# Infini-attention block with adaLN on one core: the value read-outs of a pair put in one group, the tile of row maxima padded to 128 columns

## The chip, the cores and the metric

The kernel runs on one core of a Trainium2 chip. The metric is the device time of one launch in microseconds (us). Three runs of the kernel before gave 856.10, 855.74 and 852.11 us, so the median is 855.74 us.

## The reference, cut to what matters

A transformer block over 2048 rows of width 512: layer norm with a shift and scale from a conditioning vector, an attention with 32 heads of width 16, a projection `wo`, a second layer norm, and a feed-forward part of width 1792 with a gelu. The attention works on four segments of 512 rows. Inside a segment it is a softmax over a masked score matrix; beside it a memory from the earlier segments is read out.

```python
mask = (ar[:, None] < ar[None, :]) * (-1e9)
for s in range(4):                                   # segments of 512 rows
    logits = einsum("bhqd,bhkd->bhqk", qs, ks) * scale + mask
    p = softmax(logits)
    a_dot = einsum("bhqk,bhkd->bhqd", p, vs)
    a_mem = (phi(qs) @ M) / (phi(qs) @ z + 1e-6)
    outs.append(g * a_mem + (1 - g) * a_dot)
    M, z = M + phi(ks)^T vs, z + sum(phi(ks))
```

## The kernel before, in words

The program has three stages. Stage A (about 0 to 195 us of the profile) makes q, k, v and the memory read-outs. The attention stage (about 195 to 512 us) works through the 4 x 32 = 128 matrices of scores, 512 x 512 each. The feed-forward stage takes the rest. The change touches the attention stage alone.

The attention stage runs over steps `P` = -4 to 65. A step stands for two heads (`NP` = 64 of them), and an even and the following odd step make a *pair* `Q` of four heads. For each head the scores are computed twice, on TensorE both times:

- the S parts (`s_part`, L615) give scores with rows on the partitions, only to find each row's maximum. S0 is two tiles of width 512, S1 two of 384; S2 holds two of 256 in one PSUM bank, S3 two of 128 in one bank. VectorE takes the maxima: `masked_max` (L608) for S0 to S2, an instruction that is followed by a read of the accumulator, and a plain reduction (`s_max`, L612) for S3 after the mask has been added by a matmul (`s_mask`, L645; M3 in the order). The S parts run four steps ahead of the rest.
- the T parts (`st_part`, L697) give the scores transposed, with the maximum already subtracted through three extra rows of the operand. T0 and T1 are 512 wide (one for each head), T2 and T3 384, T4 holds two of 256, T5 two of 128. ScalarE takes the exponential (L706, L717) and GpSimd zeroes the triangle (`causal`, L693). The results are the tiles `pt0` to `pt3`.

All S and T parts of a step take turns at six PSUM banks, `att0` to `att5` (`bank`, L601). A step uses twelve, so the banks come round twice in each step, and which part stands in which bank follows from the order of the tokens. A part can start only when the engine that read its bank last is done: VectorE for S, ScalarE for T.

The value read-out (`pv_part`, L722) multiplies `pt0` to `pt3` of a pair by V. Each of its four parts `j` is four matmuls onto 32 columns of the array each, side by side, and the profile shows each of these as two instructions (eight a part). They accumulate in the one bank `pv`, which ScalarE copies out (`pv_out`, L736).

Between the maxima and the T parts stand `m_rows` (L662), two small subtractions on VectorE that split the maxima in three bf16 terms in the tile `nm`; `m_put` (L668), a matmul that turns them into rows (48 columns wide); a copy to `ms` on ScalarE and a DMA of `ms` into the three extra rows of `qst`.

The projection after the attention (`wo_part`, L798) has 12 matmuls for each block of 128 rows; before the feed-forward stage they run in three runs of four pairs, one block in each pair. I call these pairs *projection pairs* and the others *plain pairs*.

The order of the work is written by hand, and every engine keeps to it. `PRM['order']` holds a string for the even and one for the odd step of each segment; `S`, `T` and `M` are parts, `c0` to `c9` are places where other work is hung in. `ap(pos, ...)` (L861) hangs work at step `pos // 10`, place `c(pos % 10)`. So `'pv'` with `[25, 0, 0, 512]` puts part 0 of pair `Q` at `20 Q + 25`, the place c5 of step `2Q + 2`. `wo`, `mput`, `pvout`, `den` and `mrows` work likewise. An L number is a line of the kernel before, as in its profile; in the changed kernel lines 40 to 592 stand three lines higher and the rest where it was.

Of the kernel before, what the change touches and what calls it, by code (L numbers as in the profile page):

```python
# [8 lines left out]
F32 = mybir.dt.float32  # L9
# [13 lines left out]
VROW = 560  # L23
EPS = 1e-5
PRM = {'order': ['S0 c0 c1 T0 T1 S1 c2 T2 c3 c4 c5 T3 S3 c6 M3 S2 c7 c8 c9 T4 T5',
# [9 lines left out]
 'turn': 2,  # L35
# [4 lines left out]
 'pvout': [35, 35, 35, 35],  # L40
 'mrows': [-19, -20, -20, -20],
 'mput': [-9, -14, -14, -14],
 'stacks': -64,
 'den': [84, 84, 84, 84],
 'dnl': 11,
# [1 line left out]
 'mix': [105, 105, 100, 103],  # L47
 'ohi': [110, 110, 110, 111],
 'olo': [110, 110, 110, 116],
 'wo': [[2, 10, 10, 10], [6, 10, 11, 11], [2, 10, 10, 11]],  # L50
 'woout': [10, 11, 11],
 'wox': [-23, -23, -23, -13],
 'mixu': 14,
# [50 lines left out]
def block_kernel(ctx: ExitStack, tc: tile.TileContext, x, wq, wk, wv, wo, betaq, betam,  # L104
                 w1, b1c, w2, b2, ccol, wmod, maskbd, mask8, out):
    nc = tc.nc
    v, act, pool, pe, sp = nc.vector, nc.scalar, nc.gpsimd, nc.tensor, nc.sync
# [6 lines left out]
    identb = per.tile([128, 128], BF16, name="identb")  # L114
# [12 lines left out]
    def copy(e, dst, src):  # L127
        if e == "a":
            act.activation(dst, src, AF.Copy)
        else:  # L130
            (v if e == "v" else pool).tensor_copy(dst, src)
# [94 lines left out]
    with ExitStack() as pa:  # L226
# [102 lines left out]
        for k in range(KB):  # L329
            for c in range(2):  # L330
                pe.matmul(ps[32 * c:32 * c + 32, :], sc[:, k:k + 1].to_broadcast([128, 32]), wms[c, k],
                          start=(k == 0), stop=(k == KB - 1))
# [6 lines left out]
        for ds in ((0,), (1, 2, 3)):  # L339
            cps = pst(f"cps{ds[0]}")  # L340
            for d in ds:
                pe.matmul(cps[:, 2 * d:2 * d + 2], row[:64, 128 * d:128 * d + 128] if d else row0, sel,
                          start=True, stop=True)
            n = slice(ds[0], ds[-1] + 1)
# [181 lines left out]
        for s in range(NSEG):  # L526
            for tok in PRM["A"][s].split():
                n = int(tok[1]) if len(tok) > 1 and tok[1].isdigit() else 0
# [53 lines left out]
    mm = psw.tile([128, 512], F32, name="mm")  # L582
# [3 lines left out]
    with ExitStack() as pb:  # L586
        sb = pb.enter_context(tc.tile_pool(name="sb", bufs=2, reuse_waits="tile"))
# [5 lines left out]
        wol = so.tile([128, KB, D], F32R, name="wol", bufs=1)  # L593

        nms, nss = {}, {}

        banks = {n: [pb_.tile([128, 512], F32, name=f"{n}{i}") for i in range(c)]
                 for n, c in (("att", 6), ("pv", 1))}
# [2 lines left out]
        def bank(n):  # L601
            turn[n] = turn.get(n, -1) + 1
            return banks[n][turn[n] % len(banks[n])]

        def s_mm(ps, P, h, i):
            pe.matmul(ps, q_of(P, h, i), k_of(P, h, 128 * (i + 1)), start=True, stop=True)  # L606

        def masked_max(dst, src, n):  # L608
            v.tensor_tensor_reduce(out=src, in0=src, in1=maskb[:, 512 - n:], scale=-1.0, scalar=-4 * NEG,  # L609
                                   op0=ALU.add, op1=ALU.min, accum_out=dst)  # L610
# [4 lines left out]
        def s_part(P, part):  # L615
            Q, p = P // 2, P % 2
            if p == 0 and part == 0:
                nms[Q] = sb.tile([128, 3, 16], F32, tag="nm", bufs=4, name=f"nm{Q}")
            nm = nms[Q][:, 0].rearrange("q (p h i) -> q p h i", p=2, h=2)
            if part < 2:  # L620
                i = 3 - part
                n = 128 * (i + 1)
                ps = [bank("att"), bank("att")]
                for h in range(2):
                    s_mm(ps[h][:, :n], P, h, i)
                for h in range(2):
                    masked_max(nm[:, p, h, i:i + 1], ps[h][:, :n], n)
            else:
                i = 3 - part
                n = 128 * (i + 1)  # L630
                ps = bank("att")
                pair = ps[:, :2 * n].rearrange("q (h n) -> q h n", h=2)
                if PRM["m"][2 * p + i]:
                    for h in range(2):
                        s_mm(pair[:, h, :], P, h, i)
                    for h in range(2):
                        masked_max(nm[:, p, h, i:i + 1], pair[:, h, :], n)
                    return
                pe.matmul(pair[:, 0, :], q_of(P, 0, i), k_of(P, 0, n), start=True, stop=False)
                pe.matmul(pair[:, 1, :], q_of(P, 1, i), k_of(P, 1, n), start=False, stop=False)  # L640
                pend.append((pair, nm[:, p, :, i:i + 1]))
# [11 lines left out]
        def q_of(P, h, i):  # L653
            return qst[P // 2 % NK][:96, 2 * (P % 2) + h, 128 * i:128 * i + 128]

        def k_of(P, h, n):
            return kst[P // 2 % NK][:96, 2 * (P % 2) + h, 0:n]

        def top(t):
            return t.bitcast(BF16).rearrange("q (n two) -> q n two", two=2)[:, :, 1]  # L660
# [6 lines left out]

        def m_put(Q):  # L668
            ns = nss.pop(Q)
            pe.matmul(mm[:48, :128], top(ns.rearrange("q c n -> q (c n)")), identb, start=True, stop=True)  # L670
            ms = sb.tile([48, 128], BF16, tag="ms", bufs=2, name=f"ms{Q}")
            copy(PRM["mse"], ms, mm[:48, :128])
            act.dma_start(qst[Q % NK][96:99], ms)
# [197 lines left out]
        for Q in range(32):  # L871
            z = Q // 8
            pv = PRM["pv"][z]
# [54 lines left out]
        for P in range(-LEAD, NP + 2):  # L928
            if P in PRM["w1at"]:
                stage_w1(2 * PRM["w1at"].index(P))  # L930
            for tok in PRM["order"][2 * min(P // 16, 3) + P % 2 if P >= 0 else 8 + P % 2].split():
                n = int(tok[1])
                if tok[0] == "S":
                    if P + LEAD < NP:
                        s_part(P + LEAD, n)
                elif tok[0] == "M":
                    s_mask()
                elif tok[0] == "T":
                    if 0 <= P < NP:
                        st_part(P, n)  # L940
                else:
                    for f, a in todo.pop((P, n), ()):
                        f(*a)
# [5 lines left out]
    with ExitStack() as pc:  # L949
        c1 = pc.enter_context(tc.tile_pool(name="c1", bufs=1, side="right", reuse_waits="tile"))  # L950
# [86 lines left out]
        c2 = pc.enter_context(tc.tile_pool(name="c2", bufs=1, reuse_waits="tile"))  # L1037
# [46 lines left out]
        for n in range(AHEAD, NSEG * FB + AHEAD):  # L1084
            s, f = divmod(n, FB)
# [77 lines left out]
```

## Time and profile before

| | us |
|---|---|
| median of the three runs | 855.74 |
| the profiled execution's own time | 852.17 |
| its span, first to last instruction | 850.4 |
| TensorE busy in the span | 811.8 (95%) |
| VectorE busy | 525.5 (62%) |
| ScalarE busy | 361.2 (42%) |
| GpSimd busy | 288.9 (34%) |

A row of a timeline gives the start, the length, the engine, the line, the operation, its tiles and shapes, and how often it was merged (x2). Matmuls overlap in the records: a matmul of width 512 lasts 0.38 us from start to end, but the next one starts 0.22 us after it. What a matmul costs TensorE is therefore read from start to start. The same holds for VectorE and ScalarE, where a read-out of the accumulator runs beside the next instruction. A row of the windows view gives a stretch of the span, and of each engine the busy time in it and the number of instructions, then the clock granted to TensorE.

### The profile page before, as it was taken

The numbers are of one execution on the slowest core, as the hardware profiler recorded it, in microseconds if no ns is written. First come the engines' busy times: TensorE is split into PE (matmuls) and PEld (weight loads), VectorE is DVE, ScalarE is ACT, GpSimd is POOL, SyncE is SP. The second block draws the span as 40 slices with busy tenths as digits, with TensorE's granted clock in tenths as the row PEclk, the third lists the DMA queues.
The fourth block names the chain that finished last, engine by engine and source line by source line (L and its number), as shares of the span: only waits on it lengthen the run. The fifth ranks groups of instructions, "written<-read, shape, count | busy, mean of one in ns | idle before, by whom it ended". The sixth has DMA issues, their size and how long they took to land.

```text
span 850.4 us, 13376 instructions
## 1 busy us (share of the span) xinstructions
PE 811.8 (95%) x4650; PEld 549.8 (65%) x4650; DVE 525.5 (62%) x1427; ACT 361.2 (42%) x730; POOL 288.9 (34%) x454
## 2 busy tenths in 40 slices
PE   6999999979999999999999899799999999999998
PEld 2777767836443455435544447688888888888887
DVE  5684676447999987897799727685442434233312
ACT  3554644522787865676687572142111211111110
POOL 1346367362367544567866561000000000000000
PEclk9999999989999999999999999899999999999999
DMA  9936747396465576666567466460030103002001
GB/s 338 325 133 228 255 166 235 108 296 199 113 176 167 150 218 189 202 191 200 174 176 217 133 182 205 155 203 30 21 99 1 49 2 99 1 0 75 26 1 49
DMA packets 83564, 123.01 MB, mean 145 GB/s; under 512 B 14116, under 2 KB 46244, under 8 KB 82984
## 3 DMA queue, kind: packets, MB, share of 16 engines
q1 hardware_dynamic: 81000, 120.19, 44.9%
q10 hardware_dynamic: 2496, 1.97, 0.7%
q8 instruction: 36, 0.59, 0.3%
q14 instruction: 32, 0.26, 0.1%
HBM read 75.60 MB, written 46.15 MB: 143 GB/s over the span
## 4 chain that ended last, share of the span: by engine, by line
PE 69%; DVE 13%; DMA 8%; issue 5%; ACT 3%; POOL 2%; SPq 0%; ACTq 0%; DVEq 0%; POOLq 0%
PE acc L1065 18%; PE f1b L984 16%; PE pv L731 6%; DVE att L609 6%; PE att L691 6%; PE att L606 4%; PE mm L804 4%; PE k L503 3%; PE q L503 2%; PE v L475 2%; PE nu L445 1%; DMA QD<-q 1%; DMA xt<-X2D 1%; DMA qst<-ms 1%; DVE nm L609 1%
## 5 line engine op out<-in xcount | busy, mean ns | idle before, releaser
L609 DVE CUSTOM_DVE_ANT_0 att<-att,maskb 128x512 f32<-128x512 f32 (+2 forms) x384 | 206.4, 580 | 13.8 <-PE att L606 11.6
L706 ACT ACTIVATE pt<-att 128x512 f32<-128x512 f32 (+1 forms) x256 | 126.0, 553 | 57.2 <-PE att L691 56.5
L987 ACT ACTIVATE gt<-f1b,b1t 128x512 f32<-128x512 f32 x56 | 38.4, 688 | 243.6 <-PE f1b L984 221.4
L694 POOL TENSOR_SCALAR_AFFINE_SELECT pt<-pt 128x256 f32<-128x256 f32 x256 | 100.2, 407 | 108.1 <-ACT pt L706 78.6
L137 DVE CAST gh<-gt 128x512 fp32r<-128x512 f32 x56 | 23.8, 426 | 156.7 <-ACT gt L987 153.8
L691 PE MATMUL att<-qst,kst 99*128 99x512 bf16 (+3 forms) x512 | 107.5, 300 | 9.1 <-DVE nm L609 3.3
L606 PE MATMUL att<-kst,qst 96*128 96x512 bf16 (+2 forms) x384 | 94.6, 327 | 1.6 <-DVE nm L613 1.2
L731 PE MATMUL pv<-pt,V 128*32 128x512 f32 (+2 forms) x992 | 88.2, 446 | 0.0
L1065 PE MATMUL acc<-w2h,gh 128*128 128x512 f32 (+1 forms) x224 | 87.2, 389 | 0.0
L1065 PE MATMUL acc<-w2l,gh 128*128 128x512 f32 (+1 forms) x224 | 86.5, 386 | 0.0
L1065 PE MATMUL acc<-w2h,gl 128*128 128x512 f32 (+1 forms) x224 | 85.9, 384 | 0.0
L691 PEld LDWEIGHTS <-kst 99*128 99x128 bf16 x512 | 43.9, 97 | 61.4 <-issue 43.9
L984 PE MATMUL f1b<-hodd,w1h 128*128 128x512 f32 x224 | 74.3, 393 | 0.0
L717 ACT ACTIVATE pt<-att 128x512 f32<-128x512 f32 (+1 forms) x128 | 57.3, 509 | 23.0 <-PE att L606 16.3
L606 PEld LDWEIGHTS <-qst 96*128 96x128 bf16 x384 | 33.2, 98 | 39.7 <-issue 24.2
L609 DVE DVE_READ_ACCUMULATOR2_ANT nm<- 128x1 f32 x384 | 54.0, 141 | 0.0
L150 POOL TENSOR_SCALAR crs<-cmv 128x4 f32<-128x4 f32 x4 | 0.9, 230 | 144.9 <-DVE cmv L147 144.8
L984 PEld LDWEIGHTS f1b<-hodd,w1h 128*128 128x128 f32 x224 | 42.0, 188 | 9.1
L1065 PEld LDWEIGHTS acc<-w2h,gl 128*128 128x128 f32 x224 | 42.1, 188 | 8.9
L1065 PEld LDWEIGHTS acc<-w2l,gh 128*128 128x128 f32 x224 | 42.0, 188 | 8.9
L1065 PEld LDWEIGHTS acc<-w2h,gh 128*128 128x128 f32 x224 | 42.1, 188 | 8.5
L731 PEld LDWEIGHTS pv<-pt,V 128*32 128x32 f32 x992 | 22.3, 109 | 38.4 <-issue 29.4
(212 smaller groups left out, 1608.1 us busy)
## 6 DMA issues: line engine op xcount, KB each, us to landing
kst<-KD SPq DMA_DIRECT2D x32, 384.0 KB
qst<-QD SPq DMA_DIRECT2D x32, 384.0 KB
TD<-ts SPq DMA_DIRECT2D x32, 256.0 KB
QD<-q SPq DMA_DIRECT2D x16, 384.0 KB
KD<-k SPq DMA_DIRECT2D x16, 384.0 KB
wm<-in_wmod SPq DMA_DIRECT2D x20, 256.0 KB
QD<-q SPq DMA_DIRECT2D x16, 256.0 KB
KD<-k SPq DMA_DIRECT2D x16, 256.0 KB
```

The source lines that it names most:

```text
L503: pe.matmul(ps, a[:, k, 128 * g:128 * g + 128], b[k], start=(n == 0), stop=(n == 11))
L606: pe.matmul(ps, q_of(P, h, i), k_of(P, h, 128 * (i + 1)), start=True, stop=True)
L609: v.tensor_tensor_reduce(out=src, in0=src, in1=maskb[:, 512 - n:], scale=-1.0, scalar=-4 * NEG, op0=ALU.add, op1=ALU.min, accum_out=dst)
L691: pe.matmul(ps, k[:99, e, 128 * j:128 * j + 128], q[:99, e, 128 * j:512], start=True, stop=True)
L694: pool.affine_select(out=t, in_=t, pattern=pattern, compare_op=ALU.is_ge, fill=0.0, base=0, channel_multiplier=-1)
L706: act.activation(pt[:, h, :], ps[:, :n], AF.Exp, scale=0.25)
L717: act.activation(pt, pv_, AF.Exp, scale=0.25)
L731: pe.matmul(ps[32 * c:32 * c + 32, lo:hi], V[4 * s + j][:, VW * hd:VW * hd + 32], pt[:, c % 2, lo - o:hi - o], start=start, stop=stop)
L804: pe.matmul(ps, a[:, 128 * b:128 * b + 128], w[:, g, :], start=(g == 0 and i == 0), stop=(g == 3 and i == 2))
L984: pe.matmul(ps, a[:, k, :], b[k], start=(i == 0), stop=(i == 11))
L987: act.activation(g, ps, AF.Gelu_apprx_tanh, bias=b1t[:, f:f + 1])
L1065: pe.matmul((mm if lo else acc[b])[:, lo:hi], a[:, c], w[:, lo:hi], start=(f == 0 and i == 0), stop=(last and i == 2))
```

## The change

Three things are changed. In every odd step the order string is replaced: T2 and T3 come first, then S1, then the places c1 to c5, and T0 and T1 behind them. The four parts of a pair's value read-out, which stood at three places (part 0 at c5 of the even step, parts 2 and 1 at c1 and c2 of the odd one, part 3 at c4; in a few segments a little otherwise), all stand at c1 to c4 of the odd step now, one behind the other. The first part of each projection block moves from c2 to c6 of the odd step, for the first and third segment; in the first segment `m_put` moves by one place. And `nm` is no longer a 48-column tile from a pool of four but one of four fixed tiles with 128 columns, whose columns from 48 on are set to zero once by GpSimd; the matmul of `m_put` takes all 128.

```diff
@@ PRM @@
-           'T0 S0 c0 c1 c2 S1 c3 T2 T3 T1 S2 c4 c5 T4 S3 M3 T5 c6 c7 c8 c9',
+           'S0 c0 T2 T3 S1 c1 c2 c3 c4 c5 T0 T1 S2 S3 T4 M3 T5 c6 c7 c8 c9',
...
- 'pv': [[[25, 0, 0, 512], [32, 1, 128, 512], [31, 2, 256, 512], [34, 3, 384, 512]],
-        [[24, 0, 0, 512], [31, 2, 256, 512], [32, 1, 128, 512], [35, 3, 384, 512]],
-        [[23, 0, 0, 512], [30, 2, 256, 512], [31, 1, 128, 512], [34, 3, 384, 512]],
-        [[25, 0, 0, 512], [30, 1, 128, 512], [31, 3, 384, 512], [35, 2, 256, 512]]],
+ 'pv': [[[31, 0, 0, 512], [32, 1, 128, 512], [33, 2, 256, 512], [34, 3, 384, 512]]] * 4,
...
- 'mput': [-9, -14, -14, -14],
+ 'mput': [-10, -14, -14, -14],
...
- 'wo': [[2, 10, 10, 10], [6, 10, 11, 11], [2, 10, 10, 11]],
+ 'wo': [[6, 10, 10, 10], [6, 10, 11, 11], [6, 10, 10, 11]],
...
@@ the attention stage @@
         nms, nss = {}, {}
+        nmt = [sb.tile([128, 8, 16], F32, name=f"nm{i}", bufs=1) for i in range(4)]
+        for t in nmt:
+            pool.memset(t[:, 3:], 0.0)
...
-                nms[Q] = sb.tile([128, 3, 16], F32, tag="nm", bufs=4, name=f"nm{Q}")
+                nms[Q] = nmt[Q % len(nmt)]
...
-            pe.matmul(mm[:48, :128], top(ns.rearrange("q c n -> q (c n)")), identb, start=True, stop=True)
+            pe.matmul(mm[:, :128], top(ns.rearrange("q c n -> q (c n)")), identb, start=True, stop=True)
```

How the order moves on TensorE is shown here for the odd step of pair 8 (its `pt16` and `pt17`) and the end of the even step ahead of it. The names are the PSUM bank written and the operands; `kst,qst` on L606 is an S part, `qst,kst` on L691 a T part, and L731 the value read-out. Before, the first row is S2 of the even step in bank `att0`; then come S0 of the odd step, parts 2 and 1 of the read-out, and S1, which takes `att0` over:

```order
L606 MATMUL att0_1978<-kst3_2055,qst3_2054 128x256
...
L606 MATMUL att5_1983<-kst3_2055,qst3_2054 128x512
L731 MATMUL pv0_1984<-pt16_2_3037,V6_145 32x256 x2
L731 MATMUL pv0_1984<-pt17_2_3088,V6_145 32x256 x2
L731 MATMUL pv0_1984<-pt16_1_3011,V5_144 32x384 x2
L731 MATMUL pv0_1984<-pt17_1_3068,V5_144 32x384 x2
...
L606 MATMUL att0_1978<-kst3_2055,qst3_2054 128x384
...
L606 MATMUL att5_1983<-kst3_2055,qst3_2054 128x256
```

Now `att0` goes from S2 of the even step to T3 of the odd step, which stands ahead of S1 and of all four parts of the read-out; behind them come T0 and T1 and only then S2:

```order
L606 MATMUL att0_1986<-kst3_2061,qst3_2060 128x256
...
L691 MATMUL att0_1986<-qst1_1760,kst1_1761 128x384
...
L606 MATMUL att2_1988<-kst3_2061,qst3_2060 128x384
L731 MATMUL pv0_1992<-pt16_0_2998,V4_143 32x512 x2
L731 MATMUL pv0_1992<-pt17_0_3075,V4_143 32x512 x2
...
L731 MATMUL pv0_1992<-pt17_3_3094,V7_146 32x128 x2
...
L691 MATMUL att4_1990<-qst1_1760,kst1_1761 128x512
...
L606 MATMUL att5_1991<-kst3_2061,qst3_2060 128x256
```

What moved: the four parts of the read-out stand between S1 and T0 in one piece, and the user of `att0` that follows the even step's S2 stands ahead of them instead of behind two of them.

On VectorE the maxima keep their order. Only the second layer norm of the second segment (its statistics, `BN_STATS`, on the tile `xt2_1` that a DMA loads) shifts against them in the last projection pairs. Before, its first instruction stood behind S0 of the even step and the projection's addition:

```order
L613 TENSOR_REDUCE nm29_5328<-att1_1979 128x2
L609 ISA att3_1981,nm30_5462<-att3_1981,maskb_65 128x512
...
L609 ISA att4_1982,nm30_5462<-att4_1982,maskb_65 128x512
...
L665 TENSOR_TENSOR nm29_5328<-nm29_5328 128x16 x2
L821 TENSOR_TENSOR xb2_0_5259<-mm_1962,xb2_0_5259 128x512
L146 BN_STATS cst1_6240<-xt2_1_6238 128x6
```

Now it stands ahead of that S0:

```order
L613 TENSOR_REDUCE nm1_1979<-att0_1986 128x2
L143 BN_STATS cst1_6216<-xt2_1_6214 128x6
L609 ISA att3_1989,nm2_1980<-att3_1989,maskb_65 128x512
...
L609 ISA att4_1990,nm2_1980<-att4_1990,maskb_65 128x512
```

What moved: two maxima and an addition that stood ahead of the first instruction on `xt2_1` now stand behind it.

8 rows, old and new, of the table PRM are left out of this document.

## The prediction

> **What bounds the kernel now.** I read the page first, then the windows by stage, then the timelines of TensorE and VectorE through one pair. The page says TensorE:
>
> ```profile
> PE 811.8 (95%) x4650; PEld 549.8 (65%) x4650; DVE 525.5 (62%) x1427; ACT 361.2 (42%) x730; POOL 288.9 (34%) x454
> ```
>
> That is a mean over three stages. The change lies in 208 to 497 us. The windows view, cut where plain and projection pairs take turns (12, 4, 4, 4, 4 and 3 pairs; columns: stretch, its length, then busy time of PE, PEld, DVE, ACT, POOL, granted clock, DMA share, GB/s), and below one plain pair:
>
> ```profile
> 208.12:306.41 98.29, 93.11 (x745) 41.80 (x746) 92.77 (x338) 72.61 (x167) 53.34 (x107) 1.00 0.53 151
> 306.41:348.97 42.56, 42.56 (x318) 22.73 (x317) 33.10 (x118) 25.40 (x60) 20.12 (x40) 1.00 0.65 195
> 348.97:383.14 34.17, 32.80 (x272) 14.61 (x271) 32.99 (x123) 25.07 (x60) 21.86 (x43) 1.00 0.66 206
> 383.14:425.49 42.35, 42.35 (x318) 22.58 (x317) 32.95 (x116) 26.14 (x62) 32.63 (x48) 1.00 0.61 186
> 425.49:458.80 33.31, 32.83 (x284) 15.96 (x283) 31.75 (x114) 27.95 (x64) 23.18 (x42) 1.00 0.64 185
> 458.80:496.64 37.84, 33.76 (x235) 17.20 (x234) 29.84 (x99) 20.35 (x47) 20.43 (x35) 0.95 0.59 172
> 290.27:298.34 8.07, 8.01 (x69) 3.58 (x68) 7.67 (x29) 6.50 (x16) 4.72 (x11) 1.00 0.59 163
> ```
>
> A projection pair (42.56 / 4 = 10.6 us) is TensorE's alone, busy without a gap; VectorE works 33.10 / 4 = 8.3 of it. A plain pair (8.07 in the last row) has two nearly full engines: TensorE 8.01, VectorE 7.67. Taking work from TensorE there can win 0.4 us at most, and only if VectorE is never left without work.
>
> **What the change takes away.** TensorE's timeline, from the plain pair:
>
> ```profile
> 290.06 0.28 PE L649 MATMUL att<-maskb,identb 128*128 128x256 bf16 x1
> 290.18 0.39 PE L606 MATMUL att<-kst,qst 96*128 96x256 bf16 x2
> ...
> 291.48 1.28 PE L731 MATMUL pv<-pt,V 128*32 128x256 f32 x16
> 292.69 0.50 PE L606 MATMUL att<-kst,qst 96*128 96x384 bf16 x2
> ...
> 293.88 0.42 PE L731 MATMUL pv<-pt,V 128*32 128x128 f32 x8
> 294.24 0.39 PE L691 MATMUL att<-qst,kst 99*128 99x256 bf16 x2
> ...
> 294.90 0.60 PE L606 MATMUL att<-kst,qst 96*128 96x512 bf16 x2
> 295.34 0.82 PE L691 MATMUL att<-qst,kst 99*128 99x512 bf16 x2
> 296.00 0.49 PE L606 MATMUL att<-kst,qst 96*128 96x384 bf16 x2
> 296.33 0.33 PE L691 MATMUL att<-qst,kst 99*128 99x384 bf16 x1
> 296.58 1.06 PE L731 MATMUL pv<-pt,V 128*32 128x512 f32 x8
> 297.58 0.34 PE L691 MATMUL att<-qst,kst 99*128 99x384 bf16 x1
> 297.75 0.22 PE L639 MATMUL att<-kst,qst 96*128 96x128 bf16 x1
> 297.81 0.22 PE L640 MATMUL att<-kst,qst 96*128 96x128 bf16 x1
> 297.96 0.24 PE L670 MATMUL mm<-identb,nm 128*48 128x128 bf16 x1
> 298.13 0.28 PE L649 MATMUL att<-maskb,identb 128*128 128x256 bf16 x1
> ```
>
> A 384-wide score matmul costs 0.16 (two from 296.00 to 296.33), but 0.25 when the read-out follows (296.33 to 296.58): entering the 32-column form costs 0.09. The last 128-wide part takes 0.36 with its eight instructions (293.88 to 294.24); by the width's share of the 512-wide part (1.00) it would be 0.25, so leaving costs about 0.11. Three visits a pair become one: 2 x 0.20 = 0.40. `m_put`, 48 columns, takes 0.15 before it and 0.17 itself (297.81, 297.96, 298.13) where a 128-wide neighbour takes 0.06 (297.75 to 297.81): padding saves 2 x 0.10 = 0.20. Together 0.6 us of TensorE a pair.
>
> The Trainium skill, "TensorEngine Tiling (Array Packing)", section Key Properties, says that a change of tiling mode, not just of tile, drains TensorE. These rows agree; where only that counted the change would win, and that is the first rival.
>
> **What it puts in the way.** The read-out in one piece takes 1.00 + 1.21 + 0.36, less two visits' 0.14 for leaving and starting, so 2.29. The order shows what now waits behind it: bank `att0` passes from S2 of the even step to T3 of the odd one, T3 stands ahead of S1, the read-out, T0, T1, S2, and TensorE goes in order. T3 must wait until VectorE has taken both maxima of the even step's S2; VectorE then has only S0 and S1 of the odd step until S2 arrives. VectorE's timeline, same pair:
>
> ```profile
> 290.45 0.42 DVE L613 TENSOR_REDUCE nm<-att 128x2 f32<-128x256 f32 x1 [0.53 <-ACT pt L706]
> 290.79 0.42 DVE L609 CUSTOM_DVE_ANT_0 att<-att,maskb 128x256 f32<-128x256 f32 x1
> 291.30 0.43 DVE L609 CUSTOM_DVE_ANT_0 att<-att,maskb 128x256 f32<-128x256 f32 x1
> 291.65 0.14 DVE L609 DVE_READ_ACCUMULATOR2_ANT nm<- 128x1 f32 x1
> 291.65 0.73 DVE L609 CUSTOM_DVE_ANT_0 att<-att,maskb 128x512 f32<-128x512 f32 x1
> 292.30 0.73 DVE L609 CUSTOM_DVE_ANT_0 att<-att,maskb 128x512 f32<-128x512 f32 x1
> ...
> 296.59 0.38 DVE L665 TENSOR_TENSOR nm<-nm 128x16 f32<-128x16 f32 x2
> 296.89 0.56 DVE L609 CUSTOM_DVE_ANT_0 att<-att,maskb 128x384 f32<-128x384 f32 x1
> 297.36 0.60 DVE L609 CUSTOM_DVE_ANT_0 att<-att,maskb 128x384 f32<-128x384 f32 x1
> 297.88 0.35 DVE L762 RECIPROCAL dn<-dn 128x32 f32<-128x32 f32 x1
> 298.52 0.43 DVE L613 TENSOR_REDUCE nm<-att 128x2 f32<-128x256 f32 x1 [0.29 <-ACT pt L706]
> ```
>
> The loop, from the second S2 maximum of an even step round to itself:
>
> - VectorE to TensorE: start to read accumulator 0.35 + 0.14 = 0.49, handover about 0.10 (the mask matmul ends at 290.06 + 0.28 = 290.34, the reduction starts at 290.45).
> - TensorE: T3 0.16, S1 0.16 + 0.25, read-out 2.29, T0 and T1 0.44 (two of 512: 294.90 to 295.34), S2 0.39 (290.18), handover 0.10. With the first leg 4.38.
> - VectorE: S2 0.51 + 0.35, S3 0.34, S0 2 x 0.65, `nm` 0.30, S1 0.47 + 0.52, S3 0.34, first S2 0.51: 4.64.
>
> The sum is 9.0 us, a floor for a plain pair, with VectorE idle for 4.38 - 0.35 - 1.30 - 0.99 = 1.7. Before, the row at 290.45 shows 0.53 idle, and the bank's next user was S1, behind parts 2 and 1 alone, with slack. The reciprocal (0.35, every second pair) lay in that idle time (297.88); now it stands inside the 4.64: +0.17 on average. A plain pair takes 9.2.
>
> **Projection pairs.** Here ScalarE's exponentials come into the loop; three in line, of widths 512, 512 and 384:
>
> ```profile
> 295.84 1.53 ACT L706 ACTIVATE pt<-att 128x512 f32<-128x512 f32 x3
> ```
>
> Before the next S2 can take `att0`, T1 of the even step must have been through TensorE and ScalarE. From T3: 0.16 + 0.41 + 2.29 + 0.44, rest of the odd step about 0.77, S0 0.44, 12 projection matmuls and T0 (2.8 + 0.2: 12 at the 0.22 of a 512-wide one are 2.6, and the two kinds of pairs differ by 10.64 - 8.07 = 2.57, to which I add 0.2 for what waits in a plain pair) make 7.5; T1's matmul 0.4, two exponentials in line about 1.1 (of the 1.53 that three take), S2 0.4, VectorE 0.5 + 0.5, handovers 0.2: about 10.5, against 10.6. So of TensorE's 0.6 only 0.1 is won.
>
> **The sum**, against the profiled execution (852.17 us: span 850.4 and 1.8 around it; the runs' median, 855.74, lies 0.4% above it). Two groups of VectorE's other work in the stage, by line and form (busy us, mean ns, idle ahead of them):
>
> ```profile
> L146 DVE BATCH_NORM_STATS2 cst<-xt 128x6 f32<-128x512 f32 x8 | 5.4, 676 | 2.6 <-DMA xt<-X2D 2.6
> L137 DVE CAST C0hh<-C0h 128x512 fp32r<-128x512 f32 x4 | 2.8, 690 | 0.0
> ```
>
> - 208 to 306: 12 pairs at 8.19; the first two have no read-out yet. 10 x (9.2 - 8.2) = +10.
> - 349 to 383: 4 x 9.2 = 36.8, and +1.4 for layer-norm statistics on VectorE's leg (two of 0.68 with their aggregation), against 34.2: +4.
> - 425 to 459: 36.8 and four casts that stand in the even step (2.8), against 33.3: +6.
> - eight projection pairs: -1.
> - 459 to 497: VectorE's stall for `xt2_1` now comes ahead of two maxima and `nm` (1.6) and TensorE idles longer: -0.5 + 3 = +2.5.
> - pairs 30 and 31 have no S parts: 2 x 0.6 less, -1.
>
> Net +20.5: 872.7, so 873.
>
> What else moves goes with one answer each. The first part of a projection block, moved off the read-out's exit, saves 0.1 for eight pairs, inside the slack. The four fills of `nm` (GpSimd, once, before the stage) cost between 0 and 4 x 0.35 = 1.4 us by the nearest small instruction in these rows, the reciprocal; GpSimd is busy for 34% of the span and nobody waits for the fills until the first maxima: 0. The wider weight load of `m_put` hides behind the matmul ahead like those of its 128-column neighbours: 0; uncovered it would be the 0.1 that a step between two such matmuls takes. In the first segment `m_put` now stands ahead of the read-out, so the DMA of `ms` gets 2 us more before T0 needs it; what TensorE waited for it there is already in the whole pairs that I replace. The copy of the read-out still stands at c5, now ahead of the exponentials of T0 and T1 instead of behind them, and the store on SP's queue goes out that much earlier; its reader comes a step later: 0. T0's tile `pt0` has three buffers and is freed by part 0, which is ahead of it in TensorE's own order: 0.
>
> If handovers are 0.05, each loop is 0.1 shorter (-2); if the stall only shifts, -3; if GpSimd or ScalarE are late in the pairs around 250, +4. That is 867 to 878 for the forecast's own bounds, say 864 to 880.
>
> **The rivals.**
>
> 1. *TensorE stays the only bound*, and every switch is won: 31 x 0.6 and 0.1 for eight pairs, 19 us, so 833. For it: projection pairs have TensorE busy throughout, and the switches are in the rows. Against it: VectorE's 7.67 of 8.07 and the bank order. It decides if S2's maxima are taken before TensorE is ready for T3: the loop would have to be under 8.07 - 0.4 = 7.7, 1.3 us shorter than I count.
> 2. *A draw.* The loop is shorter than I count (0.4 a plain pair, 18 pairs: +8) and projection pairs win most of TensorE's 0.6 (11 pairs: -6): 854.
> 3. *The clock falls.* With TensorE idle 2 us in each pair, the granted clock could drop, as it did here after a stall:
>
> ```profile
> 471.10:474.50 3.40, 1.14 (x7) 0.44 (x5) 2.98 (x11) 1.59 (x4) 2.33 (x4) 0.98 0.52 158
> 474.40:477.80 3.40, 3.20 (x19) 1.32 (x19) 2.84 (x11) 0.00 (x0) 0.00 (x0) 0.50 0.39 115
> ```
>
>  TensorE was busy for 1.14 of 3.4 us, then had half the clock for 3.4, which costs 1.7. In every second plain pair that is 9 x 1.7 = 15 on top: 888. Against it: a plain pair would still keep TensorE busy three quarters of the time. [...]
>
> **How the numbers follow.** The forecast's loop holds: 0.70 (864 to 880). Rival 1: 0.07. Rival 2: 0.08. Rival 3: 0.15. The range runs from 853 to 888 us: it takes in the forecast, most of rival 2 and half of rival 3. A measurement of this kernel can tell 0.5% (4.3 us) from no change. Faster: 0.07. Same: 0.08. Slower: 0.85.
>
> **What would show it.** Right: plain pairs of about 9.2 us; VectorE idle some 1.7 us in each, ended by S2's matmul (L606) during the read-out; T3 (L691) waiting for VectorE's L609; one visit of L731 a pair; no longer gaps around L670; projection pairs near 10.5. Wrong: plain pairs of 8 us or less with TensorE full, or a TensorE that waits for GpSimd's `pt` or a DMA instead; then the loop is not what binds.

## The result, and the profile after

| | before | after |
|---|---|---|
| median of four runs (us) | 853.92 | 894.97 |
| lowest to highest | 850.93 to 856.10 | 886.17 to 901.35 |
| the profiled execution's own time | 852.17 | 893.41 |
| its span | 850.4 | 891.7 |

The ratio is 1.0458 [1.0416, 1.0499]: slower by 4.6%. It leaves out the run of 901.35 us, which counts as slow; without it the median of the changed kernel is 893.41. I had said slower, 873 us, with 888 as the end of the range. So the direction was right, and the loss that I forecast was half of the one that came.

The engines do almost the same work as before (GpSimd has the four fills of `nm` on top) and are busy for a smaller share of a longer span:

```profile
PE 827.9 (93%) x4650; PEld 564.9 (63%) x4650; DVE 524.6 (59%) x1427; ACT 362.9 (41%) x730; POOL 288.2 (32%) x458
```

The windows by stage, cut at the same places of the work as those of before (12 plain, 4 projection, 4 plain, 4 projection, 4 plain, 3 projection pairs), and last one plain pair; the column behind POOL's is the granted clock:

```profile
210.59:323.69 113.10, 98.46 (x738) 46.81 (x737) 91.24 (x338) 73.82 (x166) 53.39 (x108) 0.95 0.46 135
323.69:369.01 45.32, 42.25 (x322) 24.15 (x321) 33.68 (x122) 24.95 (x60) 19.14 (x40) 1.00 0.56 177
369.01:413.33 44.32, 38.38 (x267) 16.93 (x265) 33.41 (x121) 25.96 (x60) 21.98 (x43) 0.85 0.51 159
413.33:458.75 45.42, 42.49 (x322) 24.13 (x321) 33.83 (x120) 25.91 (x62) 32.76 (x47) 1.00 0.57 172
458.75:499.80 41.05, 35.94 (x284) 17.66 (x282) 32.48 (x113) 27.84 (x64) 23.64 (x44) 0.96 0.53 155
499.80:539.50 39.70, 34.44 (x239) 18.10 (x241) 28.88 (x99) 20.28 (x46) 20.09 (x35) 0.91 0.48 155
234.92:243.91 8.99, 8.14 (x68) 3.92 (x67) 7.32 (x29) 6.32 (x14) 3.68 (x9) 1.00 0.50 148
```

Two things stand out against the rows of before. Projection pairs, where TensorE had no gap, now leave it 3 us in four pairs (42.25 of 45.32). And all three stretches with plain pairs, and the last one, have a clock below one: 0.95, 0.85, 0.96 and 0.91. Before, only the last had (0.95).

The lengths go from one copy to `ms` to the next. By stretch of the profiled executions, in us:

| stretch | before | after | more | forecast |
|---|---|---|---|---|
| up to the first pair (stage A and entry) | 208.12 | 210.59 | +2.5 | 0 |
| pairs 0 to 11, plain | 98.29 | 113.10 | +14.8 | +10 |
| 12 to 15, projection | 42.56 | 45.32 | +2.8 | -0.5 |
| 16 to 19, plain | 34.17 | 44.32 | +10.2 | +4 |
| 20 to 23, projection | 42.35 | 45.42 | +3.1 | -0.5 |
| 24 to 27, plain | 33.31 | 41.05 | +7.7 | +6 |
| 28 to 30, projection | 37.84 | 39.70 | +1.9 | +2.5 |
| the rest | 353.76 | 352.20 | -1.6 | -1 |
| sum | 850.4 | 891.7 | +41.3 | +20.5 |

The first row says little about the change: the same stretch took 207.43 us in e2 below, which has the changed order, and 211.92 us in e1, which has the order of before.

The single plain pairs show two kinds. Pairs 2 and 3 take 8.99 us each, 10 and 11 take 9.00 and 9.42: the forecast's 9.0 floor, and the reciprocal in every second pair. Pairs 4 to 7 take 9.89, 10.10, 11.58 and 11.14, pairs 17 to 19 take 11.03, 11.17 and 13.11, pair 26 takes 12.22. I call the second kind disturbed.

TensorE's timeline through the undisturbed pair 3 (a bracket is the idle time ahead of a row and who ended it):

```profile
234.66 0.22 PE L670 MATMUL mm<-identb,nm 128*128 128x128 bf16 x1
234.72 0.33 PE L691 MATMUL att<-qst,kst 99*128 99x384 bf16 x1
235.32 0.32 PE L691 MATMUL att<-qst,kst 99*128 99x384 bf16 x1 [0.27 <-DVE nm L609]
235.48 0.49 PE L606 MATMUL att<-kst,qst 96*128 96x384 bf16 x2
235.90 2.36 PE L731 MATMUL pv<-pt,V 128*32 128x512 f32 x32
238.19 0.60 PE L691 MATMUL att<-qst,kst 99*128 99x512 bf16 x2
...
244.31 0.32 PE L691 MATMUL att<-qst,kst 99*128 99x384 bf16 x1 [0.27 <-DVE nm L609]
```

and VectorE's for the same stretch:

```profile
234.78 0.43 DVE L609 CUSTOM_DVE_ANT_0 att<-att,maskb 128x256 f32<-128x256 f32 x1
235.13 0.14 DVE L609 DVE_READ_ACCUMULATOR2_ANT nm<- 128x1 f32 x1
...
237.46 0.14 DVE L609 DVE_READ_ACCUMULATOR2_ANT nm<- 128x1 f32 x1
239.17 0.43 DVE L609 CUSTOM_DVE_ANT_0 att<-att,maskb 128x256 f32<-128x256 f32 x1 [1.57 <-PE att L606]
...
243.77 0.43 DVE L609 CUSTOM_DVE_ANT_0 att<-att,maskb 128x256 f32<-128x256 f32 x1
```

This is the loop of the forecast, link by link. VectorE ends the second S2 maximum at 235.13 + 0.14 = 235.27; T3 starts at 235.32, 0.6 after T2 where two such matmuls need 0.16. S1, the read-out in one piece (235.90 to 238.19, 2.29, the forecast's number), T0, T1, S2 follow without a gap. VectorE, done with S1 at 237.60, stands idle 1.57 until S2 is there, and comes to the next second maximum at 243.77, 8.99 after 234.78. `m_put` costs 0.06 (234.66 to 234.72), and there is one visit of the 32-column form: both savings are there, and TensorE spends them waiting.

### The profile page after: what moved, and what is told of

Its sections match the earlier page's. It is cut to its first block, busy times and chain, and to the rows that moved or that the text cites. A ratio compares the mean times of both kernels' runs of the same rounds, so it can differ in the third digit from the quotient of the medians.

```text
span 891.7 us, 13434 instructions
## 1 busy us (share of the span) xinstructions
PE 827.9 (93%) x4650; PEld 564.9 (63%) x4650; DVE 524.6 (59%) x1427; ACT 362.9 (41%) x730; POOL 288.2 (32%) x458
## 4 chain that ended last, share of the span: by engine, by line
PE 64%; DVE 15%; issue 7%; DMA 6%; ACT 4%; POOL 3%; ACTq 1%; SPq 0%; DVEq 0%; POOLq 0%
PE acc L1065 17%; PE f1b L984 16%; PE pv L731 8%; DVE att L609 7%; PE att L691 4%; PE att L606 4%; PE mm L804 3%; PE k L500 3%; PE q L500 2%; PE v L472 2%; DVE nm L609 2%; DVE nm L613 1%; ACT pt L706 1%; DMA RD<-dn 1%; POOL kp L510 1%
## 5 line engine op out<-in xcount | busy, mean ns | idle before, releaser
L609 DVE CUSTOM_DVE_ANT_0 att<-att,maskb 128x512 f32<-128x512 f32 (+2 forms) x384 | 206.6, 579 | 67.3 <-PE att L606 51.6
L691 PE MATMUL att<-qst,kst 99*128 99x384 bf16 (+3 forms) x512 | 117.3, 304 | 27.4 <-DVE nm L609 20.3
L706 ACT ACTIVATE pt<-att 128x512 f32<-128x512 f32 (+1 forms) x256 | 124.2, 551 | 30.1 <-PE att L691 25.3
L606 PE MATMUL att<-kst,qst 96*128 96x512 bf16 (+2 forms) x384 | 101.2, 336 | 6.3 <-ACT pt L717 3.2
L731 PE MATMUL pv<-pt,V 128*32 128x512 f32 (+1 forms) x992 | 82.3, 477 | 0.0
L691 PEld LDWEIGHTS <-kst 99*128 99x128 bf16 x512 | 45.1, 98 | 52.6 <-issue 39.3
L717 ACT ACTIVATE pt<-att 128x512 f32<-128x512 f32 (+1 forms) x128 | 56.9, 505 | 25.9 <-PE att L691 16.8
L606 PEld LDWEIGHTS <-qst 96*128 96x128 bf16 x384 | 35.4, 99 | 50.3 <-issue 36.4
L731 PEld LDWEIGHTS pv<-pt,V 128*32 128x32 f32 x992 | 30.8, 117 | 55.3 <-issue 43.6
L609 DVE DVE_READ_ACCUMULATOR2_ANT nm<- 128x1 f32 x384 | 54.1, 141 | 0.0
```

Source lines behind the costliest of these rows:

```text
L691: pe.matmul(ps, k[:99, e, 128 * j:128 * j + 128], q[:99, e, 128 * j:512], start=True, stop=True)
L706: act.activation(pt[:, h, :], ps[:, :n], AF.Exp, scale=0.25)
L717: act.activation(pt, pv_, AF.Exp, scale=0.25)
L731: pe.matmul(ps[32 * c:32 * c + 32, lo:hi], V[4 * s + j][:, VW * hd:VW * hd + 32], pt[:, c % 2, lo - o:hi - o], start=start, stop=stop)
```

## The experiments

All times are medians; each ratio is to runs of the kernel before on the same chip (853.9 to 854.6 us).

| run | us | ratio | plain pairs 2, 3 | pairs 12, 13 |
|---|---|---|---|---|
| before | 853.92 | | 8.10 | 10.63 |
| changed | 894.97 | 1.0458 [1.0416, 1.0499] | 8.99 | 11.24, 11.28 |
| e1, padding alone | 850.36 | 0.9939 [0.9905, 0.9972] | 8.10 | 10.42 |
| e2, grouping alone | 897.74 | 1.0490 [1.0437, 1.0543] | 8.99 | 11.24, 11.28 |
| e3, part 0 put back | 870.01 | 1.0174 [1.0118, 1.0230] | 8.35, 8.32 | 11.00 |
| e4, T3 and S1 behind the read-out | 869.53 | 1.0147 [1.0075, 1.0218] | 8.67 | 10.88, 10.25 |
| e5, `m_put` later | 884.25 | 1.0353 [1.0322, 1.0385] | 9.00 | 10.72, 10.81 |
| e6, TensorE filled while it waits | 894.53 | 1.0445 [1.0399, 1.0491] | 9.05 | 11.24, 11.27 |
| e7, padding and one switch less | 854.21 | 0.9992 [0.9968, 1.0016] | 8.31 | 10.42 |
| e8, shorter maxima | 881.24 | 1.0312 [1.0260, 1.0364] | 8.50, 8.46 | 11.23, 11.27 |
| e9, statistics moved | 886.63 | 1.0365 [1.0308, 1.0423] | 9.00 | 11.24, 11.28 |

**e1: the padding alone**, on the kernel before:

```diff
+        nmt = [sb.tile([128, 8, 16], F32, name=f"nm{i}", bufs=1) for i in range(4)]
+        for t in nmt:
+            pool.memset(t[:, 3:], 0.0)
-            pe.matmul(mm[:48, :128], ...)
+            pe.matmul(mm[:, :128], ...)
```

> The kernel before with the padded tile of maxima alone, the order untouched. Loop theory (the loss comes from the regrouped odd step): the two switches around the maxima's matmul, 0.2 us a pair, lie on TensorE's path both in plain and in projection pairs of the kernel before, so it gains: 31 x 0.2 = 6 us, about 848. Rival (the padding itself costs, by the fills on GpSimd, the wide weight load or the fixed tiles): 855 or more.

TensorE's `m_put` (in this kernel three lines lower, L673) and the row behind it, then the windows of one plain pair and of the four projection pairs 12 to 15:

```profile
285.08 0.22 PE L673 MATMUL mm<-identb,nm 128*128 128x128 bf16 x1
285.14 0.27 PE L652 MATMUL att<-maskb,identb 128*128 128x256 bf16 x1
```

```profile
277.70:285.56 7.86, 7.70 (x69) 3.53 (x68) 7.65 (x32) 6.42 (x17) 4.92 (x11) 1.00 0.50 146
309.52:351.20 41.68, 41.68 (x318) 22.54 (x317) 33.10 (x119) 25.40 (x60) 20.16 (x40) 1.00 0.68 201
```

The step from `m_put` to the next matmul is 0.06 instead of 0.17, the wide neighbours' 0.06, and the 0.2 us forecast for it comes off the pair: 10.42 for a projection pair, 7.86 for a plain one of the second segment. It is the one version that beats both kernels, by 4.2 us from the 854.6 of before on the same chip, against the 6 expected. In pairs 2 and 3 nothing came off: they take 8.10 as before, with TensorE busy for 7.94 of it and VectorE for 7.44 to 7.47 in both kernels. Neither was full there, and which wait held these pairs was not followed.

**e2: the grouping alone** (the changed kernel with `m_put` back at 48 columns):

```diff
-            pe.matmul(mm[:, :128], top(ns.rearrange("q c n -> q (c n)")), identb, ...)
+            pe.matmul(mm[:48, :128], top(ns[:, :3].rearrange("q c n -> q (c n)")), identb, ...)
```

> The changed kernel with the maxima's matmul back at 48 columns, the rest as changed. Loop theory: that matmul stands in the even step, where TensorE waits anyway, so the 0.2 us a pair that come back are hidden: 890 to 900, as the changed kernel. Rival (TensorE's own work is still what counts): 6 us more, 901, and the plain pairs at 9.2 instead of 9.0.

Pair 2, the first one with a read-out, and a projection pair, at the places of 8.99 and 11.24 in the changed kernel:

```profile
222.56:231.56 9.00, 8.36 (x68) 3.88 (x68) 7.33 (x29) 6.30 (x15) 3.16 (x9) 1.00 0.50 141
322.76:334.00 11.24, 10.88 (x86) 6.41 (x85) 8.80 (x33) 6.46 (x16) 5.33 (x10) 1.00 0.74 217
```

The same lengths with a dearer `m_put`. What is worth 0.2 us a pair while TensorE is the bound is worth nothing while it waits for others.

**e3: part 0 back at c5 of the even step**, which takes its 1.0 us out of the piece in the loop:

```diff
- 'pv': [[[31, 0, 0, 512], [32, 1, 128, 512], [33, 2, 256, 512], [34, 3, 384, 512]]] * 4,
+ 'pv': [[[25, 0, 0, 512], [31, 1, 128, 512], [32, 2, 256, 512], [34, 3, 384, 512]]] * 4,
```

> The changed kernel with part 0 of the read-out back at c5 of the even step, parts 1 to 3 in one piece in the odd step. Loop theory: TensorE's leg of the loop loses 0.9 us, the loop is 8.1 to 8.2 us and hardly binds: plain pairs 8.2, TensorE's idle share and with it the halvings of the clock go, 860 to 868 in all. Rival (the place of T0 and T1, or the clock alone): plain pairs stay at 9.0 and the time at 885 or more.

```profile
227.31:235.67 8.36, 7.94 (x68) 3.74 (x67) 7.51 (x29) 6.18 (x16) 3.16 (x9) 1.00 0.56 155
```

VectorE's wait for S2 in that pair:

```profile
230.61 0.43 DVE L609 CUSTOM_DVE_ANT_0 att<-att,maskb 128x256 f32<-128x256 f32 x1 [0.71 <-PE att L606]
```

The wait falls from 1.57 to 0.71, so 0.86 of the part's 1.0 is gone from the loop; the pair shortens by 0.63, since VectorE's own work in it is 0.2 longer (7.51 against 7.32). The pair (8.2 expected) and the whole time (860 to 868 expected) both end a little above what was expected. The whole kernel gains 25 us, more than the 18 plain pairs at 0.6 (11) and eight projection pairs at 0.25 (2): most of the disturbed pairs are gone too (pairs 6 and 7 take 9.05 and 7.67), and of the six stretches at half clock in the attention stage one is left.

**e4: T3 and S1 behind the read-out**, so that T3 no longer holds it up:

```diff
-           'S0 c0 T2 T3 S1 c1 c2 c3 c4 c5 T0 T1 S2 S3 T4 M3 T5 ...',
+           'S0 c0 T2 c1 c2 c3 c4 c5 T3 S1 T0 T1 S2 S3 T4 M3 T5 ...',
```

> The changed kernel with T3 and S1 of the odd step moved behind the read-out, which stays in one piece. Loop theory: T3, the next user of the bank of the even step's S2, no longer stands ahead of the read-out, so the read-out runs while VectorE works off the even step: plain pairs 8.1 to 8.4, few halvings of the clock, 860 to 870. Rival (one long read-out starves VectorE wherever it stands): plain pairs 9 us or more, 890 or more.

TensorE, then VectorE, and the pair's window:

```profile
222.88 0.79 PE L691 MATMUL att<-qst,kst 99*128 99x256 bf16 x4 [0.23 <-DVE nm L609]
...
224.25 2.36 PE L731 MATMUL pv<-pt,V 128*32 128x512 f32 x32
226.55 0.34 PE L691 MATMUL att<-qst,kst 99*128 99x384 bf16 x1
```

```profile
227.08 0.57 DVE L609 CUSTOM_DVE_ANT_0 att<-att,maskb 128x384 f32<-128x384 f32 x1 [1.24 <-PE att L606]
```

```profile
224.19:232.86 8.67, 8.13 (x68) 3.91 (x67) 7.33 (x29) 6.32 (x14) 3.17 (x9) 1.00 0.50 141
```

The whole time is within the expected 860 to 870, but the pair is longer than the expected 8.1 to 8.4: a second loop of the same kind stands behind the first. T3 has no wait left (226.55, straight behind the read-out). Now S1 is late, VectorE idles 1.24 for it, and T4 and T5 of the even step wait for VectorE (222.88) ahead of the same read-out. So with 2.3 us of read-out in one piece, a bank that VectorE frees for TensorE ahead of it and gets back behind it closes such a loop; e4 shows this for one more place.

**e5: `m_put` four places later** in segments 1 to 3, and with it the copy to `ms` and the DMA that ScalarE issues:

```diff
- 'mput': [-10, -14, -14, -14],
+ 'mput': [-10, -10, -10, -10],
```

> The changed kernel with the maxima's matmul at c0 of the odd step in all segments, as it is in the first one. ScalarE issues the DMA of the rows itself, and this holds its queue for 0.73 us right ahead of the exponentials of T4 and T5, for which S1 of the odd step waits. Theory (this queue is what made the projection pairs 11.2 us instead of the 10.5 forecast): projection pairs 10.8, plain pairs unchanged at 9.0 to 9.4, 4 to 6 us less in all, 890. Rival (the projection pairs are held by VectorE alone): 11.2 as before.

First the changed kernel's projection pair 13, TensorE and then ScalarE (ACTq is ScalarE's queue issuing a DMA):

```profile
336.20 0.32 PE L691 MATMUL att<-qst,kst 99*128 99x384 bf16 x1 [0.53 <-DVE nm L609]
336.71 0.60 PE L606 MATMUL att<-kst,qst 96*128 96x384 bf16 x2 [0.19 <-ACT pt L717]
337.23 2.36 PE L731 MATMUL pv<-pt,V 128*32 128x512 f32 x32
...
344.01 0.61 PE L691 MATMUL att<-qst,kst 99*128 99x512 bf16 x2
...
347.23 0.32 PE L691 MATMUL att<-qst,kst 99*128 99x384 bf16 x1 [0.29 <-DVE nm L609]
347.99 0.32 PE L606 MATMUL att<-kst,qst 96*128 96x384 bf16 x1 [0.43 <-ACT pt L717]
```

```profile
346.21 0.27 ACT L126 ACTIVATE ms<-mm 48x128 bf16<-48x128 f32 x1
346.51 0.73 ACTq L673 DMA_DIRECT2D qst<-ms  x1
347.34 0.87 ACT L717 ACTIVATE pt<-att 128x512 f32<-128x512 f32 x2 [0.86 <-DVE nm L609]
```

S1 comes round from 336.71 to 347.99, 11.28, the length of this pair. It waits for the exponential of T4 (L717), which stands on ScalarE's queue behind the copy to `ms` and the DMA's issue, 0.27 and 0.73 us. The bracket at 347.34 names VectorE, of which this exponential needs nothing; it starts 0.10 behind the end of the issue (346.51 + 0.73 = 347.24). With both moved, TensorE's rows in the same place, and the window of the four pairs:

```profile
333.00 0.32 PE L691 MATMUL att<-qst,kst 99*128 99x384 bf16 x1 [0.47 <-DVE nm L609]
333.17 0.49 PE L606 MATMUL att<-kst,qst 96*128 96x384 bf16 x2
```

```profile
321.84:364.70 42.86, 41.02 (x317) 23.83 (x316) 33.12 (x119) 24.95 (x58) 18.51 (x39) 1.00 0.61 181
```

S1 follows T3 after 0.17, and the four pairs take 42.86 instead of 45.32. That was expected, and it is the DMA's issue, with the copy, that held S1; `m_put` itself moved with them. The whole kernel gains about 10 us, more than the 4 to 6 expected; 4.6 of it lie in the eight projection pairs. What is left is T3's wait for VectorE: about the forecast's 10.5, at 10.7.

**e6: work for TensorE while it waits.** The matmul of T2 in the odd step is issued four times. The theory tried was that TensorE's steady idle share lets the granted clock fall:

```diff
-                st_mm(ps[:, :n], P, h, j)
+                for _ in range(4 if P % 2 and part == 2 else 1):
+                    st_mm(ps[:, :n], P, h, j)
```

> The changed kernel with the first matmul of T2 in the odd step issued four times instead of once, to the same result: 0.48 us more of TensorE's work a pair, at the place where it waits 0.6 us for VectorE ahead of T3. Theory (the clock is halved after a stretch of 3.4 us with TensorE busy for under two thirds, and the loop does not see the filler): pairs as long as before, at most two halvings in the attention stage instead of six, 10 to 15 us faster, 880 to 885. Rival (the halvings have another cause): as many halvings, the same time or up to 5 us more, 895 to 900.

Pairs 2 and 3 together, and one window ahead of a stretch at half clock (from 384.1):

```profile
224.62:242.72 18.10, 16.94 (x142) 8.43 (x141) 14.65 (x57) 12.62 (x29) 6.88 (x17) 1.00 0.49 135
380.70:384.10 3.40, 1.74 (x9) 0.67 (x7) 3.33 (x9) 2.49 (x6) 2.55 (x6) 1.00 0.83 261
```

The undisturbed pair is filled to 0.94 and only 0.06 longer than in the changed kernel (9.05), so the filler lay in the wait. But there are as many stretches at half clock in the attention stage, six, and they follow windows in which TensorE was busy for 1.74 to 2.29 of 3.4 us; the second row is one of them. That theory fell. The clock does not fall for the wait that every pair has; it falls after a disturbed pair.

**e7: e1 with one switch less**, part 3 moved up behind the two middle parts (the same in all four segments). Pure TensorE accounting gives 0.2 us a pair:

```diff
- 'pv': [[[25, 0, 0, 512], [32, 1, 128, 512], [31, 2, 256, 512], [34, 3, 384, 512]],
+ 'pv': [[[25, 0, 0, 512], [32, 1, 128, 512], [31, 2, 256, 512], [32, 3, 384, 512]],
```

> The kernel before with the padded tile and part 3 of the read-out moved up to c2, behind parts 2 and 1, so two visits of the read-out a pair instead of three; order strings untouched. Theory (switches are worth their 0.2 us where TensorE sets the pace and no loop is closed): 0.2 us less in projection pairs and up to 0.2 in plain ones, 844 to 848, against 850 with padding alone. Rival (any longer read-out starves VectorE): 850 or more, plain pairs above 7.9.

The plain pair 8, at the place of e1's 7.86, and VectorE's wait for S1 in pair 2, first e1's and then this kernel's (lines stand three lower in both, so L612 is the maximum and L609 the S part):

```profile
280.80:288.88 8.08, 7.75 (x69) 3.71 (x68) 7.68 (x30) 6.51 (x17) 4.79 (x11) 1.00 0.48 137
```

```profile
229.25 0.57 DVE L612 CUSTOM_DVE_ANT_0 att<-att,maskb 128x384 f32<-128x384 f32 x1 [0.30 <-PE att L609]
```

```profile
228.76 0.57 DVE L612 CUSTOM_DVE_ANT_0 att<-att,maskb 128x384 f32<-128x384 f32 x1 [0.51 <-PE att L609]
```

This is not what was expected: the plain pairs are 0.21 longer, and projection pairs, where TensorE is full, win 0.05 at most. S1 stands behind the longer piece, and VectorE waits those 0.2 us more. So even this half-way grouping gives back what the switch saves.

**e8: VectorE's leg shortened.** The maxima of S0 in even steps go over 256 of 512 columns; half of that maximum is left out:

```diff
+                    m = 256 if p == 0 and part == 0 else n
-                    masked_max(nm[:, p, h, i:i + 1], ps[h][:, :n], n)
+                    masked_max(nm[:, p, h, i:i + 1], ps[h][:, n - m:n], m)
```

> The changed kernel with the two maxima of S0 in even steps taken over the last 256 of 512 columns only (half of that maximum is left out): VectorE's leg of the loop is 2 x 0.27 = 0.54 us shorter, TensorE's work the same. Loop theory: plain pairs with a read-out go from 9.0 to 8.45, projection pairs stay, about 9 us less in all and fewer halvings. Rival (TensorE, ScalarE or GpSimd hold the plain pairs): 9.0 as before.

```profile
221.68:238.64 16.96, 15.91 (x135) 7.83 (x134) 13.61 (x57) 12.28 (x29) 6.45 (x17) 1.00 0.55 152
```

Two pairs take 16.96 instead of 17.98: VectorE's time is in the loop nearly one for one there (0.51 a pair for 0.54). In the second segment's plain pairs I expected the same and got 8.80 to 8.83, 0.4 less than the changed kernel's mean of 9.21. In every second one of them S1 stands 0.45 behind T3 (298.29 and 298.74) instead of 0.16, behind an exponential that starts at 298.09, 0.11 after the issue of the DMA ends (297.23 + 0.75). So ScalarE's queue seems to be the next limit; no run moved the DMA in this kernel. Projection pairs did not move, which fits e5: ScalarE's queue holds S1 in them.

**e9: the layer-norm statistics out of VectorE's leg.** In the changed kernel the four of them follow each other at short distances through pairs 17 to 19: the first ahead of an even step's S0, the second between S0 and S1 of an odd step, the third in an even step, the last behind S1 of an odd step. Here each stands behind S1 of an odd step, where VectorE waits 1.57 us for the read-out, one in each of four pairs, so that two of them leave for the projection pairs 20 and 21:

```diff
- 'ln': [312, 339, 374, 408],
+ 'ln': [312, 352, 414, 418],
...
- 'lnd': [11, 10],
+ 'lnd': [20, 10],
```

> The changed kernel with its layer-norm statistics moved, in the segments where they run beside attention, from the even steps to the place c2 of the odd steps, behind the row maxima of S1, where VectorE waits for TensorE's read-out anyway. If the extra time of the plain pairs 16 to 19 (44.3 us in the changed kernel for four pairs, 36.0 by the loop alone) is VectorE's other work standing on the loop, with the halved clock that follows its long waits, these four pairs take 37 to 39 us, the halvings at 388.0 and 401.6 go, and the kernel takes 880 to 886 us. Rival: those pairs are long for another reason (the loop's waits themselves, the clock): then they stay at 43 to 45 us and the kernel at 890 to 896.

Pairs 16 to 19, at the place of the 44.32 at clock 0.85:

```profile
367.27:404.10 36.83, 32.47 (x267) 15.34 (x265) 30.87 (x117) 25.79 (x59) 20.59 (x41) 1.00 0.62 187
```

They take 9.01, 9.42, 9.00 and 9.41: the bare loop, at full clock. 7.5 us are gone by moving four pieces of 0.87 us, and pairs 20 and 21, which take two of them up, stay at 11.24 and 11.50. One thing came along: the two subtractions of pair 17 took 1.37 us beside GpSimd in the changed kernel (387.30) and take 0.38 here (384.76), so the run does not tell the statistics from that collision. The whole kernel is at 886.63, just above the 880 to 886 expected.

## Why the prediction was right, and where it was wrong

**Right: the mechanism and the plain pair.** The loop of 9.0 with 0.17 for the reciprocal was forecast; 8.99 and, over two pairs, (9.00 + 9.42) / 2 = 9.21 were measured. The legs were right and not only the sum: from the second S2 maximum to the next S2 on VectorE 4.39 measured (234.78 to 239.17) against 4.38, and 4.60 from there (to 243.77) against 4.64. e3 and e8 changed one link each (TensorE's and VectorE's) and the undisturbed pair followed: by 0.63 of the 0.86 by which VectorE's wait fell, and by 0.51 of 0.54. e2 and e6 changed TensorE's work outside the loop and the pair stayed within 0.06. Rivals 1 and 2 (TensorE alone, a draw) are out, and so is the idea that the mode switches decide: the padding pays by itself (e1), but joining two visits of the read-out does not (e7).

**Right by size alone: the last pairs and the tail**, +1.9 against +2.5 and -1.6 against -1. No run tested their mechanism, and the last pairs hold two windows at half clock where before had one, so this may be luck.

**Wrong: the projection pairs.** The step "So of TensorE's 0.6 only 0.1 is won" should have been: 0.6 is lost. Between T3 and the read-out I had 0.16 + 0.41 = 0.57; pair 13 has 337.23 - 336.20 = 1.03, and in the next pair S1 alone stands 0.76 behind T3 (347.23 to 347.99) where I had 0.16. The other links are as forecast: read-out to T1 7.0 against 6.94 (337.23 to 344.01 + 0.22), T1 to T3 3.0 against 3.1. (My terms in fact add up to 10.6 and not to the 10.5 that I wrote, so even by them nothing was won.) I had counted S1 as free to follow T3; it waited for ScalarE, whose DMA issue of 0.73 us stood in no term of mine, and parts 2 and 1 of the read-out, which had given S1 time for that, were being moved away from ahead of it. Over the eight pairs: +5.8 instead of -1, so 6.8 us.

**Wrong: VectorE's other work, and rival 3's price and cause.** The sum had VectorE's other work at its bare length: +1.4 for the statistics in pairs 16 to 19, which with what they brought on measured 7.5 there (44.32 against e9's 36.83), and nothing for the subtractions `nm` beside GpSimd in pairs 4 to 7. The +4 that I had set aside if GpSimd is late around 250 us is near what came in the first stretch (+14.8 against +10), but it stood in the bounds and not in the sum. I gave the falling clock 0.15 and tied it to the idle time of every pair. It came without that: the windows of 3.4 us around the stretches at half clock in the changed kernel, TensorE's busy time first:

```profile
261.70:265.10 3.40, 2.10 (x15) 1.00 (x18) 3.37 (x13) 1.58 (x5) 3.40 (x5) 1.00 0.51 165
265.10:268.50 3.40, 3.40 (x24) 1.06 (x20) 1.48 (x6) 1.27 (x3) 2.04 (x4) 0.50 0.03 8
...
384.60:388.00 3.40, 2.13 (x10) 0.77 (x8) 3.37 (x10) 2.65 (x7) 2.38 (x5) 1.00 0.89 275
388.00:391.40 3.40, 2.68 (x12) 1.66 (x13) 3.33 (x12) 1.83 (x5) 2.63 (x5) 0.50 0.49 151
```

The chain of a disturbed pair can be read at 260 us, GpSimd, VectorE, TensorE:

```profile
260.35 1.26 POOL L852 TENSOR_TENSOR wol<-wor,woh 128x512 fp32r<-128x512 f32 x1
```

```profile
260.72 1.28 DVE L665 TENSOR_TENSOR nm<-nm 128x16 f32<-128x16 f32 x2
```

```profile
262.59 0.79 PE L691 MATMUL att<-qst,kst 99*128 99x256 bf16 x4 [0.90 <-DVE nm L609]
```

The two subtractions `nm`, 0.38 us in the prediction's rows (296.59), take 1.28 while GpSimd subtracts; that is on VectorE's leg of the loop, so the pair lengthens, TensorE waits 0.90 more, is busy 2.10 of a window of 3.4, and then has half the clock for the next. The collision is not new: one of the subtractions takes 1.13 to 1.15 us in the kernel before too (at 245.1, 254.0, 262.7 and 271.4 us), where pairs 4 to 6 take 8.70 to 8.95 instead of 8.10 and no window of these pairs runs at half clock. In the changed kernel pairs 4 to 7 are 0.9 to 2.6 us longer than pairs 2 and 3. In pair 17 the statistics (385.24) stand ahead of such a collision (387.30); e9 took out both, and with them both stretches at half clock of pairs 17 to 19. The Trainium skill, "SBUF — State Buffer", section "SBUF: two separate sides", has VectorE and GpSimd share a pair of ports, which an instruction of VectorE with two inputs in SBUF and one of GpSimd that reads SBUF hold against each other to their end. These rows agree: GpSimd ends at 260.35 + 1.26 = 261.61, and the first subtraction, 0.93 us long, at 261.65.

In the attention stage ten windows of 3.4 us ran at half clock (one before). At 1.7 us each the nine more are worth at most 15 us; that is an estimate from the rows, and an upper one, since the loop has legs on VectorE that the clock does not touch. Between runs the changed kernel itself shows the same: 896.53 us with a mean clock of 0.969 and 886.17 with 0.981. So of the 41 us 20.5 are the forecast's and 6.8 the projection pairs'. Another 12.7 (4.8 + 6.2 + 1.7) lie in the three plain stretches beyond the forecast, with the disturbed pairs and their clock, and 2.5 ahead of the first pair, where e1 and e2 show the same spread; the last two rows take off 1.2. How the 12.7 divide between VectorE's longer leg and the clock was not separated; in pairs 16 to 19 e9 took both away together.

The range failed with rival 3: I let it reach to half of that case, and left out that half clock can come on top of the forecast's loop from causes that the loop brings out, VectorE's odd work.

## What to carry to other kernels

When work of two engines is regrouped, follow each buffer that changes hands round to itself and add up both engines' legs: a loop that closes at 9.0 us is not shortened by a saving on one engine outside it, here 0.6 us a pair by the forecast (e1 measured 0.2 of it; the other 0.4 was not measured alone). Then put every instruction of each queue in the loop on that sum, the issue of a DMA too, and ask what cover the moved work had given to others. And once an engine's slack is gone, odd work on it (statistics, a subtraction beside GpSimd) costs more than it did: move it into the new wait, as e9 does.

## What was not expected of the hardware

- Half the clock does not take an idle window. It followed windows of 3.4 us in which TensorE was busy for 2.10 and 2.13 us, and in the kernel before one from 471.0 us without an idle stretch of TensorE above 1.42 us. The Trainium skill, "TensorE: Matmul & The Clock Gate", section "What's actually happening", has the clock fall after at least one idle window of about 3.4 us. By these rows a window that is three fifths busy can be enough, though the ends of the matmuls in the records are modelled and the border is not sharp.
- The issue of one small DMA holds ScalarE's queue for 0.73 us (346.51 to 347.24), and the next exponential, at 347.34, starts only then.
- Padding a matmul of 48 columns to 128 took 0.2 us off it and its neighbours in pairs where TensorE was full (e1), 0.6% of the kernel.

How unsharp the border of the first point is shows in this window of the kernel before, which was followed by full clock:

```profile
269.60:273.00 3.40, 2.10 (x16) 0.57 (x13) 3.37 (x12) 2.78 (x7) 2.36 (x5) 1.00 0.72 222
```

Cut on the grid on which the windows at half clock lie, the profiles of all eleven kernels have 1065 windows at full clock between about 195 and 545 us. All 29 in which TensorE was busy for less than 2.08 us were followed by half clock, and none in which it was busy for more than 2.47 us; in between both occur.
